# The last output store of a fused attention and MLP block, split by partitions over two DMA queues

## Chip, cores and metric

The kernel runs on one core of a Trainium2 chip. The metric is the device time of one execution in microseconds (us). The kernel before takes 205.89 us (median of three runs, 205.84 to 206.03).

## What is computed

The input `x` has 2048 tokens (S) of width 640 (D), in bf16. It is normalised, and the output is the sum of the input, a linear attention block with 32 heads and an MLP with 1536 hidden columns (F):

```python
xn = _layernorm(x, axis=-1)
return x + _A_ref(xn, A_wqkv, A_wo) + _B_ref(xn, B_w1, B_b1, B_w2, B_b2)
...
# _A_ref
q, k, v = qkv[0], qkv[1], qkv[2]
phi = lambda t: jnp.where(t > 0, t + 1, jnp.exp(t)) + 1e-6
pq, pk = phi(q), phi(k)
kv = jnp.einsum("bhsd,bhse->bhde", pk, v)
z = jnp.einsum("bhsd->bhd", pk)
num = jnp.einsum("bhqd,bhde->bhqe", pq, kv)
den = jnp.einsum("bhqd,bhd->bhq", pq, z)[..., None] + 1e-6
o = num / den
return (lambda x, *d: x.transpose(*d))(o, 0, 2, 1, 3).reshape(B, S, D) @ wo
...
# _B_ref
h = jnp.einsum("bsd,df->bsf", x, w1) + b1
h = _gelu(h)
return jnp.einsum("bsf,fd->bsd", h, w2) + b2
```

## The kernel before

Tokens are worked on in 16 tiles (`t`) of 128, four tiles to a chunk (`c`). The stages follow one another on TensorE: layer norm and the hidden layer of the MLP (line 408 and around), the features of the keys (563, 569), their products with the tokens (596, 605), the features of the queries (648), the matrices that join attention and output weights (658, 702), the denominators (712), and the output.

The output stage is what the change touches. For a tile, `out_mm` (matmuls on line 768) sums 17 products into one PSUM bank: 12 blocks of the hidden layer (`HG`) with `W2`, and 5 blocks of the query features (`PQ`) with the joined matrices (`Msb`). The columns of the output are cut in two: the main part, columns 0 to 511 (`MW` = 512), has the tokens on the partitions; the remainder, 128 columns, is computed transposed for a whole chunk (`rem_mm`, line 779; `rem_done`, line 784), turned back by a DMA transpose and stored from SP. `main_done` (lines 790 to 794) adds the residual to the main part of a tile with one VectorE addition (line 792) into one of two slots of `out_sb`, which is stored by a DMA on ACT's queue, 128 KB.

The order is written out by hand. The remainder of the last chunk comes before its tiles, so that tile 15 is last. Its main part is cut in two pieces, columns 0 to 383 and 384 to 511, each with its own 17 matmuls in a bank of its own, its own addition (line 847) and its own store (line 850). Both stores are issued on SP's queue.

A small recorder, `Planner`, keeps for each engine the list of its operations in program order, and for each buffer part the event of its last writer and of its readers; it makes an engine wait for just those events that it has not yet been seen to know. Each DMA has a semaphore of its own, complete at 16. Every DMA is issued by the helper `dma`, on line 261, or `dma_t`, on line 264, so all issues carry these two line numbers. After the last store, lines 852 to 854 make SP wait for the last DMA of ACT's queue and the last three of its own:

```python
for q, n in ((s_, 1), ("sync", 3)):
    for ev in [ev for (waits, fns, ev, dma_) in Pl.records[q] if dma_][-n:]:
        Pl.wait_event("sync", ev)
```

These waits appear under line 108. After them all engines meet in a closing barrier, shown under the last line of the block, 861. The name `s_` is ACT ("scalar"), and `P` is 128.

Of the kernel before, what the change touches and what calls it, by code (L numbers as in the profile page):

```python
# [7 lines left out]
P = 128  # L8
# [104 lines left out]
def bass_parallel_sum__linear_attn_block__dense_activation_gelu__prompt_kernel(  # L113
# [27 lines left out]
    with contextlib.ExitStack() as es:  # L141
# [46 lines left out]
        out_sb = W1f[:, 2 * DT * D:2 * DT * D + 2 * D].rearrange("p (s d) -> p s d", s=2)  # L188
# [21 lines left out]
        def bank(b, lo=0, hi=512):  # L210
            return ps[:, b * 512 + lo: b * 512 + hi]
# [39 lines left out]
        ov = out.rearrange("b s d -> (b s) d")  # L251
# [5 lines left out]
        s_ = "scalar"  # L257
        pe = "tensor"

        def dma(eng, dst, src, writes, reads=()):  # L260
            Pl.ins(eng, lambda e: e.dma_start(dst, src), reads=reads, writes=writes, dma=True)  # L261
# [12 lines left out]
        for i, (lo, hi) in enumerate(((0, XA), (XA, D))):  # L274
# [21 lines left out]
               reads=[r_ident], writes=[r_ident])  # L296
# [155 lines left out]
        for b in range(6):  # L452
            Pl.ins(pe, lambda e, b=b: e.matmul(
                bank(b), nc.const_aps.tensor(1.0, [P, P], BF16), pm[:].broadcast_to((P, 512)), start=True, stop=False),
                reads=[r_pm], writes=[B_[b]])
# [102 lines left out]
        for c in range(NC):  # L558
            ts = range(c * CH, c * CH + CH)
            cc = slice(c * CW, (c + 1) * CW)  # L560
            for t in ts:
# [4 lines left out]
                    reads=r_xnT[t] + [r_Wk], writes=[B_[b]])  # L566
# [5 lines left out]
                reads=sum((r_xnT[t] for t in ts), []) + [r_Wk], writes=[B_[b]])  # L572
            phi(bank(b), b, 1, PKT[:, cc], r_PKT[c], [])
            dma_t("sync", PK[:, c * CH:(c + 1) * CH, MW:D], PKT[:, cc], [r_PKr[c]] + sum((r_x[t] for t in ts), []),
                  reads=[r_PKT[c]])
# [12 lines left out]
        for k in range(DT):  # L588
            for i in range(DT):
                Pl.ins(g, lambda e, k=k, i=i: e.tensor_copy(plain(Wqkv[:, k, D:2 * D], i), parts(Wqkv[:, k, 0:D], i)),  # L590
                       reads=[r_Wq], writes=[r_Wk, r_WqP])
# [173 lines left out]
        def out_mm(t, lo, hi, w0, w1):  # L765
            seq = seq_of(t)
            for i in range(lo, hi):
                Pl.ins(pe, [(lambda e, i=i, x=x, bk=bk: e.matmul(  # L768
                    bank(bk, 0, x[1] - x[0]), seq[i][0], seq[i][1][:, x[0]:x[1]],
                    start=(i == 0), stop=(i == NS - 1))) for x, bk in zip(w0, w1)],  # L770
                    reads=seq[i][2], writes=[B_[bk] for bk in w1], mark=(i in (JT - 1, NS - 1)))
# [68 lines left out]
        t = NT - 1  # L840
        xb(t)
        tok = slice(t * P, (t + 1) * P)
        for i, (lo, hi, b) in enumerate([(0, 3 * P, bb[1]), (3 * P, MW, bb[2])]):
            r_o = R_("ol%d" % i)
            out_mm(t, 0, NS, [(lo, hi)], [b])
            s = t % 2
            Pl.ins(v, lambda e, lo=lo, hi=hi, b=b: e.tensor_tensor(  # L847
                out=out_sb[:, s, lo:hi], in0=bank(b, 0, hi - lo), in1=x_res[:, t, lo:hi], op=ALU.add),
                reads=[B_[b], r_xb[t]], writes=[r_o] + ([r_out[s]] if i == 0 else []))
            dma("sync", ov[tok, lo:hi], out_sb[:, s, lo:hi], [], reads=[r_o])  # L850

        for q, n in ((s_, 1), ("sync", 3)):
            for ev in [ev for (waits, fns, ev, dma_) in Pl.records[q] if dma_][-n:]:
                Pl.wait_event("sync", ev)

# [35 lines left out]
```

## Time and profile before

| what | before |
|---|---|
| median of three runs | 205.89 us (205.84 to 206.03) |
| the profiled execution's own time | 206.18 us |
| its span, first to last instruction | 204.5 us |
| granted TensorE clock | 1.000 |
| TensorE matmul busy | 200.7 us (98%) |
| VectorE busy | 108.8 us (53%) |
| ScalarE (ACT) busy | 71.3 us (35%) |
| last store, columns 384 to 511 of tile 15: issue to landing | 1.5 us, 32 KB |
| store before it, columns 0 to 383: issue to landing | 1.6 us, 96 KB |
| store of a main part on ACT's queue: issue to landing | 1.7 us, 128 KB |

The profile is one execution. Its own time is the span plus what lies around it. PE is TensorE, DVE is VectorE, ACT is ScalarE, SP is the engine that only issues DMAs and waits; ACTq and SPq are the queues of DMA-issuing instructions of these engines. The times of rows in a timeline count from the start of the span. "Issue" is the instruction that starts a DMA; its data move afterwards on 16 DMA engines, and "landing" is when its semaphore is complete. In the table of DMA queues, q1 holds the transfers that SP issued, q10 those that ACT issued.

### The profile page before, as it was taken

The page shows a single profiled execution, that of the slowest core. Times are in us where ns is not written, and L with a number is a line of the kernel's source. Part 1 is how long each engine was busy: PE and PEld are TensorE (multiplying, and loading weights), DVE is VectorE, ACT ScalarE, POOL GpSimd, SP SyncE. Part 2 cuts the span into 40 slices and gives each one's busy share as a digit, 9 for nine tenths or more (in the row PEclk, how much of TensorE's full clock was granted, in tenths as well). Part 3 has the DMA queues.
Part 4 walks back from the last instruction along what each step waited for, and adds up shares of the span by engine and source line. Part 5 has one row for each costly group of instructions (what it writes and reads, how often), then busy time and mean ns, then how long its engine had stood idle before and what let it go on. Part 6 is the DMA issues. An engine that isn't in the chain of part 4 may idle for free.

```text
span 204.5 us, 3358 instructions
## 1 busy us (share of the span) xinstructions
PE 200.7 (98%) x1238; PEld 104.6 (51%) x1238; DVE 108.8 (53%) x238; ACT 71.3 (35%) x144; POOL 33.5 (16%) x84
## 2 busy tenths in 40 slices
PE   8899999999999999999999999999999999999995
PEld 3899884444444444444546444544444444444443
DVE  3588764000007889399748888834634723513131
ACT  2269995666676555121154464500000000000000
POOL 3245637300000001897000200000000000000000
PEclk9999999999999999999999999999999999999999
DMA  5997595799800111100050001239985511102301
GB/s 170 370 265 93 116 179 101 216 329 353 282 7 0 26 26 26 29 0 0 0 99 2 0 0 21 86 52 201 326 217 131 140 42 52 51 26 51 79 29 51
DMA packets 35769, 21.70 MB, mean 106 GB/s; under 512 B 22696, under 2 KB 35112, under 8 KB 35752
## 3 DMA queue, kind: packets, MB, share of 16 engines
q1 hardware_dynamic: 31696, 17.86, 33.8%
q10 hardware_dynamic: 4056, 3.61, 6.6%
q8 instruction: 10, 0.16, 0.4%
q14 instruction: 7, 0.06, 0.1%
HBM read 13.08 MB, written 2.62 MB: 77 GB/s over the span
## 4 chain that ended last, share of the span: by engine, by line
PE 96%; DMA 2%; SPq 0%; DVE 0%; issue 0%
PE ps L768 29%; PE ps L408 19%; PE ps L648 11%; PE ps L596 8%; PE ps L563 8%; PE ps L779 7%; PE ps L439 3%; PE ps L423 3%; DMA W<-in_B_w_dram 2%; PE ps L605 2%; PE ps L569 2%; PE ps L702 1%; PE ps L658 1%; PE ps L712 1%; SPq L261 0%; DVE W L847 0%
## 5 line engine op out<-in xcount | busy, mean ns | idle before, releaser
L768 PE MATMUL ps<-W,HG 128*128 128x512 bf16 (+2 forms) x204 | 43.9, 367 | 0.0
L408 PE MATMUL ps<-xnT,W 128*128 128x512 bf16 (+1 forms) x225 | 39.1, 336 | 0.0
L768 PEld LDWEIGHTS ps<-W,HG 128*128 128x128 bf16 x204 | 19.5, 98 | 22.2 <-ACT Msb L684 0.2
L551 ACT ACTIVATE ek<-ps 128x512 bf16<-128x512 f32 x40 | 23.8, 597 | 19.6 <-DVE PQ L554 9.3
L408 PEld LDWEIGHTS ps<-xnT,W 128*128 128x128 bf16 x225 | 21.9, 98 | 16.8 <-issue 0.3
L412 ACT ACTIVATE HG<-ps,b1c 128x512 bf16<-128x512 f32 (+1 forms) x45 | 26.3, 670 | 11.3 <-PE ps L408 10.8
L552 DVE TENSOR_SCALAR ek<-ek 128x512 bf16<-128x512 bf16 x40 | 11.4, 286 | 28.3 <-ACT ek L551 28.3
L792 DVE TENSOR_TENSOR W<-ps,xnT 128x512 bf16<-128x512 f32 x15 | 10.4, 691 | 24.9 <-PE ps L768 19.6
L648 PE MATMUL ps<-xnT,Wqkv 128*128 128x512 bf16 x100 | 21.9, 379 | 0.0
L768 PE MATMUL ps<-Msb,PQ 128*128 128x512 bf16 (+2 forms) x85 | 19.6, 366 | 0.0
L563 PE MATMUL ps<-Wqkv,xnT 128*128 128x512 bf16 x80 | 17.9, 379 | 0.0
L596 PE MATMUL ps<-xPK,xn_tm 128*128 128x512 bf16 x80 | 17.4, 379 | 0.0
L590 POOL COPY Wqkv<-Wqkv 128x128 bf16<-128x128 bf16 x25 | 13.5, 540 | 22.4 <-PE ps L569 20.9
L357 DVE BATCH_NORM_STATS2 stats<-xPK 128x6 f32<-128x320 bf16 (+2 forms) x32 | 13.9, 478 | 5.3 <-DMA xPK<-in_A_x_dram 5.3
L648 PEld LDWEIGHTS ps<-xnT,Wqkv 128*128 128x128 bf16 x100 | 9.6, 98 | 11.5
L554 DVE SCALAR_TENSOR_TENSOR PQ<-ps,ek 128x512 bf16<-128x512 f32 x20 | 13.8, 691 | 2.1
L768 PEld LDWEIGHTS ps<-Msb,PQ 128*128 128x128 bf16 x85 | 8.1, 98 | 9.2
L596 PEld LDWEIGHTS ps<-xPK,xn_tm 128*128 128x128 bf16 x80 | 7.8, 98 | 9.4
L563 PEld LDWEIGHTS ps<-Wqkv,xnT 128*128 128x128 bf16 x80 | 7.8, 98 | 9.4
L554 DVE SCALAR_TENSOR_TENSOR xPK<-ps,ek 128x512 bf16<-128x512 f32 x16 | 11.1, 692 | 1.7
L619 DVE TENSOR_TENSOR Msb<-Msb,xPK 128x640 f32<-128x640 f32 x14 | 11.6, 826 | 0.5
L367 POOL TENSOR_TENSOR rstd<-aggr,mhalf 128x1 f32<-128x1 f32 x16 | 10.0, 623 | 7.4 <-DVE aggr L365 7.4
(77 smaller groups left out, 156.6 us busy)
## 6 DMA issues: line engine op xcount, KB each, us to landing
Wqkv<-in_A_wqkv_dram SPq DMA_DIRECT2D x3, 800.0 KB, 6.8
xnT<-in_A_x_dram SPq DMA_DIRECT2D x4, 512.0 KB, 6.5
W<-in_B_w_dram SPq DMA_DIRECT2D x5, 384.0 KB, 5.6
W<-in_B_w_dram SPq DMA_DIRECT2D x1, 1920.0 KB, 13.4
out_dram<-W ACTq DMA_DIRECT2D x15, 128.0 KB, 1.7
xn_tm<-rden ACTq DMA_DIRECT2D x12, 128.0 KB, 3.8
xPK<-in_A_x_dram SPq DMA_DIRECT2D x4, 320.0 KB, 6.9
Wo<-in_A_wo_dram SPq DMA_DIRECT2D x8, 160.0 KB, 8.9
```

Of the source, the lines that this page charges most:

```text
L357: Pl.ins(v, lambda e: e.bn_stats(stats[:, s, 6 * h:6 * h + 6], x_in[:, t, lo:hi]), reads=[r_x[t][min(h, len(r_x[t]) - 1)]], writes=[r_stat ...
L408: Pl.ins(pe, [(lambda e, k=k: e.matmul(bank(b, 0, w), W1[:, k, jb * P:(jb + 1) * P], xnT[:, k, tok], start=(k == 0), stop=(k == DT - 1))) ...
L412: Pl.ins(s_, lambda e: e.activation(HG[:, jb, tok], bank(b, 0, w), ACT.Gelu_apprx_tanh, bias=b1c[:, jb:jb + 1]), reads=[B_[b], r_b1c], wri ...
L551: Pl.ins(s_, lambda e: e.activation(e2, src, ACT.Exp), reads=br, writes=[r_ek[s]])
L554: Pl.ins(v, lambda e: e.scalar_tensor_tensor(out=d2, in0=src, scalar=0.0, in1=e2, op0=ALU.max, op1=ALU.add), reads=br + [r_ek[s]], writes= ...
L563: Pl.ins(pe, [(lambda e, k=k, b=b, t=t: e.matmul(bank(b), xnT[:, k, t * P:(t + 1) * P], Wqkv[:, k, D:D + MW], start=(k == 0), stop=(k == D ...
L590: Pl.ins(g, lambda e, k=k, i=i: e.tensor_copy(plain(Wqkv[:, k, D:2 * D], i), parts(Wqkv[:, k, 0:D], i)), reads=[r_Wq], writes=[r_Wk, r_WqP])
L596: Pl.ins(pe, lambda e, t=t, b=b, f=f, i=i: e.matmul(bank(b), xn_tm[:, t, f * P:(f + 1) * P], PK[:, t, 0:MW], start=(i == 0), stop=(i == NT ...
L619: Pl.ins(v, lambda e, t=t: e.tensor_tensor(out=zsum, in0=zsum, in1=PK[:, t, :], op=ALU.add), reads=[r_PK[t], r_PKr[t // CH], r_zsum], writ ...
L648: Pl.ins(pe, [(lambda e, k=k, j=j, b=b: e.matmul(bank(b), Wqkv[:, k, D + j * P:D + (j + 1) * P], xnT[:, k, cc], start=(k == 0), stop=(k == ...
L768: Pl.ins(pe, [(lambda e, i=i, x=x, bk=bk: e.matmul(bank(bk, 0, x[1] - x[0]), seq[i][0], seq[i][1][:, x[0]:x[1]], start=(i == 0), stop=(i = ...
L779: Pl.ins(pe, lambda e, i=i: e.matmul(bank(b), seq[i][0], seq[i][1], start=(i == 0), stop=(i == NS - 1)), reads=seq[i][2], writes=[B_[b]], ...
```

## The change

The store of the last piece (columns 384 to 511 of tile 15) becomes two stores of 64 partitions each: partitions 0 to 63 on SP's queue, partitions 64 to 127 on ACT's queue. Both read the result of the same addition. The store of columns 0 to 383 stays on SP's queue, whole. The waits at the end take the last two DMAs of ACT's queue, so that the new one is among them.

```diff
                 reads=[B_[b], r_xb[t]], writes=[r_o] + ([r_out[s]] if i == 0 else []))
-            dma("sync", ov[tok, lo:hi], out_sb[:, s, lo:hi], [], reads=[r_o])
-
-        for q, n in ((s_, 1), ("sync", 3)):
+            if i == 0:
+                dma("sync", ov[tok, lo:hi], out_sb[:, s, lo:hi], [], reads=[r_o])
+            else:
+                for q, r0 in (("sync", 0), (s_, P // 2)):
+                    dma(q, ov[t * P + r0:t * P + r0 + P // 2, lo:hi], out_sb[r0:r0 + P // 2, s, lo:hi], [], reads=[r_o])
+
+        for q, n in ((s_, 2), ("sync", 3)):
             for ev in [ev for (waits, fns, ev, dma_) in Pl.records[q] if dma_][-n:]:
                 Pl.wait_event("sync", ev)
```

On each engine the program is otherwise the same: SP's last issue has 64 rows instead of 128, ACT's queue has one more issue of 64 rows at its end, and the other engines' instructions are unchanged.

## The prediction

> **What bounds the kernel now.** I read the chain of waits first. TensorE carries it nearly to the end:
>
> ```profile
> PE 96%; DMA 2%; SPq 0%; DVE 0%; issue 0%
> ...
> 187.44 14.73 PE ps L768 x85
> 202.17 0.02 issue
> 202.19 0.29 DVE W L847
> ```
>
> The change touches no matmul, so only what follows the last matmul can move. Next, the timeline of the last 3.5 us (columns: start us, us, engine, line, operation):
>
> ```profile
> 201.25 0.56 DVE L847 TENSOR_TENSOR W<-ps,xnT 128x384 bf16<-128x384 f32 x1 [1.74 <-PE ps L768]
> 201.71 0.44 PE L768 MATMUL ps<-Msb,PQ 128*128 128x128 bf16 x5
> 201.83 1.02 SPq L261 DMA_DIRECT2D out_dram<-W  x2
> 202.19 0.29 DVE L847 TENSOR_TENSOR W<-ps,xnT 128x128 bf16<-128x128 f32 x1 [0.39 <-PE ps L768]
> ```
>
> The two SP issues are shown as one row. The view of line 261 gives the length of one, and when the second starts:
>
> ```profile
> L261 SPq DMA_DIRECT2D out_dram<-W x2: 344/344/345, 201.8 to 202.5; - x2
> ```
>
> So the first runs from 201.83 to 202.18, and the second ends at 201.83 + 1.02 = 202.85 and starts 0.344 earlier, at 202.51, within 0.03 us of the end of the last addition at 202.48. The data of the stores are not in these rows; a table by stage over the tail has them (last two columns: share of the 16 DMA engines, GB/s):
>
> ```profile
> 202.67:203.12 0.45, 0.00 (x0) 0.00 (x0) 0.00 (x0) 0.00 (x0) 0.00 (x0) 1.00 0.68 219
> 203.12:203.35 0.23, 0.00 (x0) 0.00 (x0) 0.00 (x0) 0.00 (x0) 0.00 (x0) 1.00 0.00 0
> 203.35:203.62 0.27, 0.00 (x0) 0.00 (x0) 0.00 (x0) 0.00 (x0) 0.00 (x0) 1.00 0.56 122
> 203.62:204.45 0.83, 0.00 (x0) 0.00 (x0) 0.00 (x0) 0.00 (x0) 0.00 (x0) 1.00 0.00 0
> ```
>
> The first active stretch is the 96 KB store, the second the 32 KB store. The wait at the end shows when SP learns that each has landed:
>
> ```profile
> L108 SPq EVENT_SEMAPHORE  x2: 17/22/28, 203.5 to 204.0; - x2
> ```
>
> The tail of the store that the change splits is therefore: issue at 202.51; 0.84 us without a packet, up to 203.35; 0.27 us of packets, up to 203.62; 0.37 us until SP passes the last wait at 203.99; 0.46 us of closing barrier up to 204.45. Only 0.27 us of these 1.94 us is movement of data; the rest does not depend on how many bytes one queue carries.
>
> **What the Trainium skill says.** (1) "DMA: Bandwidth & Descriptors", section "Rules for kernel authors": two transfers to disjoint partition halves are not worth it, since both spread over the same 16 DMA engines. No run here shows this shape yet; the trace agrees in that all 16 engines take part in the 32 KB store (its 128 rows show as 144 packets: the rows and 16 small ones that end each engine's share). (2) The same page, section "Why a DMA increments its semaphore by 16 and not by 1": the number of engines is the largest divisor, up to 16, of the slowest dimension; 64 rows still give 16 engines, four rows on each. (3) "Perfetto Trace Analysis", section "DMA Instruction — HWDGE (DVE, Sync)": the two issuing sequencers share one descriptor generator, which one holds at a time. The trace has a pair that agrees in part, used below.
>
> **The change part by part.** The sum is made against the profiled execution: 206.18 us, of which 204.45 us is the span and 1.73 us lies around it. It is 0.29 us above the median of 205.89 us, so I add differences to the median.
>
> *SP's half.* The SP instruction stays where it was, with 64 rows in place of 128. Its issue of 0.344 us hardly depends on rows: a store of 512 rows takes 0.377 to 0.387 us. From these, 64 rows fewer save under 0.01 us. The issue itself has not been what the end waits for, since packets start 0.84 us after its start. SP's half should then start packets at 203.35 as before.
>
> *ACT's half, added.* ACT has been idle since its last store:
>
> ```profile
> 199.21 0.34 ACTq L261 DMA_DIRECT2D out_dram<-W  x1
> ```
>
> That one was released by the addition that ended at 198.48 + 0.69 = 199.17, so ACT starts 0.04 us after its addition where SP took 0.03: the new issue starts at 202.52, 0.01 behind SP's, and ends at 202.86. No instruction waits behind it on ACT but the closing barrier, which ACT then reaches at 202.9 instead of 199.6; SP reaches it at 204.0, so this is covered by 1.1 us. Alone, an ACT store's first packet comes at 200.05, 0.84 us after its issue, the same as on SP. At the same time as SP's, it may be later. The trace has one such pair among the stores, at 191.80 and 191.87:
>
> ```profile
> 191.80 0.38 SPq L261 DMA_DIRECT2D out_dram<-xPK  x1
> 191.87 0.34 ACTq L261 DMA_DIRECT2D out_dram<-W  x1
> ```
>
> Neither issue is lengthened. The DMA queues show which one's packets come first, in the stretches 192.60 to 192.84 and 192.60 to 192.86:
>
> ```profile
> q1 hardware_dynamic: 90, 0.02, 40.8%
> ```
>
> ```profile
> q1 hardware_dynamic: 105, 0.03, 43.9%
> q10 hardware_dynamic: 3, 0.00, 3.3%
> ```
>
> q1 is SP's, q10 ACT's. Until 192.84 there is nothing from ACT; its first packets come at 192.85, 0.98 us after its issue and 0.14 us after SP's first (192.71). The pair at the very start of the kernel, issued within 0.01 us of each other at 0.81, says the same: SP's first packet at 1.85, ACT's at 1.99, again 0.14 us later. So the price of a simultaneous issue is bounded by 0 (two generators) and 0.14 us (the second of the pair waits its turn). I take 0.14, since both pairs show it, and keep 0 as the other end.
>
> *The packets*, read one by one from the trace's packet records. Within the 32 KB store each of 16 engines moves 8 rows; the first engine is done at 203.47 (0.11 us after the first packet), the last at 203.61. The spread of 0.14 us between engines is there for stores of 96 and 128 KB too (0.16 us), so I keep it. Four rows instead of eight take 0.06 us instead of 0.11. ACT's half: first packet 203.35 + 0.14 = 203.49, last 203.49 + 0.06 + 0.14 = 203.69, against 203.61 before: +0.08 us. SP's half is over by 203.55 and does not decide. On any one engine SP's four rows are gone by the time ACT's four arrive (0.06 against 0.14 us), so they don't queue on each other. With no offset between the halves an engine would move the same eight rows plus one more small closing packet of 0.01 us, and the first packet may come 0.01 earlier with fewer rows: between -0.01 and +0.01 us.
>
> *The end.* The landing follows the last packet by 0.36 us and does so for the 128 and 96 KB stores also (0.35); kept. SP now waits for five semaphores instead of four. As built, the second of its two wait instructions takes the two halves together, and the first one the older stores, so no instruction is added: 0. The wait that is added for the older ACT store has been over since 200.9 (199.21 + 1.7 us to its landing). The barrier keeps its 0.46 us.
>
> *Sum.* +0.08 us: the span goes to 204.53, the profiled execution to 206.26, and the median to 205.89 + 0.08 = 205.97 us.
>
> **The rivals.** *A, offset (the forecast):* 205.97, as above, within 0.2% (0.41 us, about what a measurement of this kernel can tell from no change).
>
> *B, both halves at once:* the skill's lock does not show because each issue needs the generator only briefly. Both queues start at 203.35 and finish with the old store, 205.88 to 205.90, or down to 205.84 if an engine moves the rows of its two queues side by side, so that each saves 0.05 us. The pair at 191.80 and the one at 0.81 speak against it; two records are few. It can't become a gain beyond 0.2%: even if all 0.27 us of packets vanished, the time would be 205.62, which is still within it. That the split does nothing at all is this case too.
>
> *C, the lock lengthens an issue:* slower than before. While ACT was issuing its broadcasts around 140 us, SP's loads took far longer to issue:
>
> ```profile
> L261 ACTq DMA_DIRECT2D xn_tm<-rden x5: 635/825/1369, 139.2 to 142.4; - x5
> L261 SPq DMA_DIRECT2D xnT<-in_A_x_dram x3: 368/822/855, 139.5 to 140.9; - x3
> ```
>
> One took 0.368 us, two took 0.82 to 0.86. If one half has to wait like this at its issue, its packets and its landing are later by 0.855 - 0.368 = 0.49 us, and the median is 205.89 + 0.49 = 206.38, or 206.46 with A's 0.08. It decides "slower" from 0.41 us on, so only a delay of nearly this size counts. Against it: DMA engines[...] were full of broadcasts and loads at 140 us and are empty at 202.5, and neither issue of the pair at 191.80 (0.377 and 0.344 us) was lengthened.
>
> **How the numbers follow.** A 0.72, B 0.20, C 0.08. The likeliest is A, so 205.97 is the forecast. A's own range is +0.02 to +0.15 us (offset smaller for fewer rows, or the whole 0.14 without the rows saved); B adds the lower end, -0.05 us. The three runs of before span 0.19 us; I allow half of that, 0.10, below, and above it the 0.14 by which the highest run exceeds the median. Lower end: 205.89 - 0.05 - 0.10 = 205.74; upper end: 205.89 + 0.15 + 0.14 = 206.18. C is left outside, with A and B's own tails no more than 2 in 10. Chances: faster by over 0.2% is only measurement, 0.02; slower by over 0.2% is C, 0.08 less the part of it under 0.41 us, so 0.07; within 0.2% 0.91.
>
> **What would show it.** In the profile after: SP's and ACT's issue both at 202.5 on this clock, each of about 0.34 us (right for A and B; over 0.8 for one of them is C). Packets of q1 from 0.84 us after the issue, those of q10 0.14 us later (A) or together (B). Last packet 0.08 us later against the end of the last addition (A) or within 0.02 (B). Two wait instructions on SP as before, and 0.46 us from the last to the end of the span. The prediction is wrong if the gap from the last packet to the landing is not 0.36 us with two queues, if ACT starts late because it was idle for 3 us, or if the matmuls before the tail move at all.

## The result and the profile after

The changed kernel is slower: 206.85 us (median of six runs, 206.76 to 207.16) against 206.00 for the kernel before beside it (six runs, 205.84 to 206.40). The ratio is 1.0040, 95% interval 1.0027 to 1.0053, so 0.56 to 1.09 us. The forecast was 205.97 us, with a range up to 206.18; the time lies above it.

The profiled execution took 206.82 us with a span of 205.1 us, against 206.18 and 204.5. The chain of waits is less tidy than before, because 17 matmul records are missing from this trace (1221 matmuls in place of 1238) and the chain goes round the gaps by other engines; its last piece is the same work with the same end, TensorE up to 202.2 us:

```profile
PE 72%; DVE 19%; DMA 4%; issue 2%; ACT 1%; DVEq 0%
...
196.16 6.05 PE ps L768 x44
```

The end of the last addition moved by 0.04 us, from 202.49 to 202.53. In the profiles of the kernels below it lies anywhere between 201.99 (e8) and 202.83 (g4), so this shift says nothing of the change. The rest of the 0.62 us by which the span grew lies behind it. The timeline of the tail, and the view of line 261 there (minimum, median and maximum length in ns):

```profile
201.87 1.24 SPq L261 DMA_DIRECT2D out_dram<-W  x2
202.23 0.29 DVE L847 TENSOR_TENSOR W<-ps,xnT 128x128 bf16<-128x128 f32 x1 [0.39 <-PE ps L768]
202.56 0.57 ACTq L261 DMA_DIRECT2D out_dram<-W  x1
```

```profile
L261 SPq DMA_DIRECT2D out_dram<-W x2: 345/451/557, 201.9 to 202.6; - x2
L261 ACTq DMA_DIRECT2D out_dram<-W x1: 575/575/575, 202.6 to 202.6; - x1
```

The 96 KB store is issued in 0.345 us as before. The two halves take 0.557 and 0.575 us, where the whole store took 0.344. The table by stage shows the same delay in the data (last two columns: share of the DMA engines, GB/s):

```profile
202.70:203.16 0.46, 0.00 (x0) 0.00 (x0) 0.00 (x0) 0.00 (x0) 0.00 (x0) 1.00 0.67 214
203.16:203.75 0.59, 0.00 (x0) 0.00 (x0) 0.00 (x0) 0.00 (x0) 0.00 (x0) 1.00 0.00 0
203.75:203.99 0.24, 0.00 (x0) 0.00 (x0) 0.00 (x0) 0.00 (x0) 0.00 (x0) 1.00 0.33 69
203.99:204.02 0.03, 0.00 (x0) 0.00 (x0) 0.00 (x0) 0.00 (x0) 0.00 (x0) 1.00 0.00 0
204.02:204.26 0.24, 0.00 (x0) 0.00 (x0) 0.00 (x0) 0.00 (x0) 0.00 (x0) 1.00 0.34 69
204.26:205.08 0.82, 0.00 (x0) 0.00 (x0) 0.00 (x0) 0.00 (x0) 0.00 (x0) 1.00 0.00 0
```

The silence between the 96 KB store and the last piece was 0.23 us and is 0.59. The queues in the stretch from 203.74 to 204.03 say whose packets came first:

```profile
q1 hardware_dynamic: 80, 0.02, 27.7%
q10 hardware_dynamic: 1, 0.00, 0.3%
```

SP's half (q1, 64 rows and 16 closing packets) is complete before ACT's (q10) begins. And SP's last wait, which began at 204.0 and lasted 28 ns, now begins when SP's half has landed and is held 268 ns for ACT's:

```profile
L108 SPq EVENT_SEMAPHORE  x2: 28/148/268, 203.5 to 204.4; - x2
```

In terms of the prediction's sum, counted from the end of the last addition: SP's first packet at 1.23 us instead of 0.87 (+0.36); ACT's first packet 0.27 behind it; packets of one half 0.22 us instead of 0.26 (-0.04); landing 0.36 after the last packet, as before (counted, here and below, from the start of that packet, a closing one of 0.01 us). Together +0.59, and the span does end 2.55 us after the addition where it ended 1.97 us after it.

### The profile page after: what moved, and what is told of

Read it like the earlier page. It is cut to its first block, busy times and chain, and to the rows that moved or that the text cites. A ratio compares the mean times of both kernels' runs of the same rounds, so it can differ in the third digit from the quotient of the medians.

```text
span 205.1 us, 3342 instructions
## 1 busy us (share of the span) xinstructions
PE 200.2 (98%) x1221; PEld 105.0 (51%) x1238; DVE 108.8 (53%) x238; ACT 71.3 (35%) x144; POOL 33.4 (16%) x84
## 4 chain that ended last, share of the span: by engine, by line
PE 72%; DVE 19%; DMA 4%; issue 2%; ACT 1%; DVEq 0%
PE ps L768 29%; PE ps L408 19%; PE ps L779 7%; PE ps L563 6%; DVE Msb L619 6%; DVE PQ L554 3%; PE ps L439 3%; PE ps L423 3%; PE ps L648 3%; DVE ek L552 2%; DVE xPK L554 2%; DMA Msb<-Msb 2%; DMA xPK<-Msb 1%; DMA xPK<-in_A_x_dram 1%; PE ps L569 1%
```

## The experiments

Two questions were open: why the issues and first packets of the halves are late, and why ACT's comes 0.27 us after SP's. The table gives, for all kernels, how long an issue takes, and then times in us counted from the end of the last addition, from the packet and landing records of their profiles. The last two columns are how much later than before the span ends in this count ("tail"), and the difference of the medians of the runs, each against the kernel before as run beside it. The ratios in the text are estimates from all these runs, and not quotients of the medians: for g4 they differ most (1.0001, and +0.18 us between the medians).

| kernel | issue SP; ACT | first packet SP; ACT | last landing | end of span | tail | medians |
|---|---|---|---|---|---|---|
| before | 0.34; - | 0.87; - | 1.48 | 1.97 | | |
| changed | 0.56; 0.58 | 1.23; 1.50 | 2.08 | 2.55 | +0.59 | +0.85 |
| e4, SP half only | 0.56; - | 1.23; - | 1.81 | 2.31 | +0.34 | +0.47 |
| e1, both on SP | 0.56, 0.59; - | 1.23, 1.87; - | 2.44 | 2.92 | +0.96 | +1.02 |
| e6, whole stores as a pair | 0.34; 0.35 | 0.95; 0.89 | 1.85 | 2.34 | +0.37 | +0.38 |
| e2, by columns | 0.35; 0.37 | 0.87; 0.94 | 1.63 | 2.10 | +0.14 | +0.13 |
| e7, 96 and 32 rows | 0.35; 0.38 | 0.88; 0.96 | 1.65 | 2.11 | +0.14 | +0.29 |
| e8, four quarters | 0.35, 0.42; 0.38, 0.45 | 0.87, 1.34; 0.91, 1.38 | 2.08 | 2.61 | +0.65 | +0.88 |
| e3, late ACT | 0.55; 0.55 | 1.23; 1.53 | 2.11 | 2.57 | +0.61 | +0.71 |
| changed, again | 0.56; 0.58 | 1.23; 1.50 | 2.07 | 2.54 | +0.58 | +0.69 |
| g1, whole, unmarked | 0.56; - | 1.23; - | 1.85 | 2.35 | +0.38 | +0.42 |
| g2, 96 and 32, unmarked | 0.63; 0.62 | 1.30; 1.57 | 2.10 | 2.56 | +0.59 | +0.82 |
| g3, 80 and 48 rows | 0.35; 0.38 | 0.88; 0.95 | 1.63 | 2.11 | +0.14 | +0.13 |
| g4, 120 and 8 rows | 0.41; 0.32 | 0.93; 0.84 | 1.51 | 2.00 | +0.04 | +0.18 |

Each tail lies within the 95% interval of its own comparison, which reaches 0.14 to 0.28 us to either side. The medians are on average 0.1 us above the tails, and in the first comparison 0.26 us; that part is not explained.

**First theories: a collision of two issues, or the 64 rows.** The rival that the prediction had named, a lock that lengthens an issue, would need two issues at once. So one half was left out.

```diff
-                for q, r0 in (("sync", 0), (s_, P // 2)):
+                for q, r0 in (("sync", 0),):
...
-        for q, n in ((s_, 2), ("sync", 3)):
+        for q, n in ((s_, 1), ("sync", 3)):
```

> Only SP's half of the last piece is stored (64 rows); the store of partitions 64 to 127 of the last 128 columns of tile 15 is left out. Theory 'rows': a 64-row store is dearer by itself. Then its issue takes 0.56 us as in the changed kernel, its first packet comes 1.20 us after the issue, and the time is 0.3 us above the kernel before. Theory 'collision': two issues at the same moment hold each other up, and 64 rows cost nothing. Then the issue takes 0.34 us, the first packet comes after 0.84 us, and the time is that of the kernel before, less up to 0.05 us.

```profile
L261 SPq DMA_DIRECT2D out_dram<-W x2: 344/450/557, 201.6 to 202.3; - x2
```

```profile
202.90:203.50 0.60, 0.00 (x0) 0.00 (x0) 0.00 (x0) 0.00 (x0) 0.00 (x0) 1.00 0.00 0
203.50:203.73 0.23, 0.00 (x0) 0.00 (x0) 0.00 (x0) 0.00 (x0) 0.00 (x0) 1.00 0.35 72
```

With nothing on ACT the issue of 64 rows still takes 0.557 us, and the silence is still 0.60 us. The ratio is 1.0022 (1.0013 to 1.0032). A store of half the data is slower than the whole one: the collision is out as the cause of the 0.36 us.

Both halves on one queue:

```diff
-                for q, r0 in (("sync", 0), (s_, P // 2)):
+                for q, r0 in (("sync", 0), ("sync", P // 2)):
...
-        for q, n in ((s_, 2), ("sync", 3)):
+        for q, n in ((s_, 1), ("sync", 4)):
```

> Both 64-row halves on SP's queue, one after the other, so that no two issues meet. 'Rows': each issue 0.56 us, the second half's first packet 0.56 + 1.20 us after the addition; the time is 0.9 us above the kernel before. 'Collision': each issue 0.34 us, second half 0.34 us later than the old store, the time 0.3 us above.

Issues of 0.557 and 0.586 us, one after the other; ratio 1.0042 (1.0030 to 1.0055), +1.02 us between the medians and +0.96 of tail, where "rows" had said 0.9.

A pair of whole 128-row stores, the 96 KB one held back to the second addition (this edit is shown against the kernel before; the waits are those of the changed kernel):

```diff
-            dma("sync", ov[tok, lo:hi], out_sb[:, s, lo:hi], [], reads=[r_o])
+            if i == 0:
+                r_o0 = r_o
+            else:
+                dma("sync", ov[tok, 0:lo], out_sb[:, s, 0:lo], [], reads=[r_o0, r_o])
+                dma(s_, ov[tok, lo:hi], out_sb[:, s, lo:hi], [], reads=[r_o])
```

> No split: the 96 KB store (SP) is held back to the second addition, so that it and the 32 KB store (now on ACT) of 128 rows each are issued at the same moment. 'Collision': both issues about 0.56 us, first packets at 1.2 us (SP) and 1.47 us (ACT) after the issue, the time 0.6 us or more above the kernel before. 'Rows': both issues 0.34 us, first packets at 0.84 and 0.98 us, the time 0.15 to 0.3 us above.

The issues started 0.04 us apart and took 0.344 and 0.349 us. First packets came 0.86 us (ACT) and 0.88 us (SP) after their issues. Ratio 1.0019 (1.0011 to 1.0026), a little above what "rows" had expected: with both stores on the way at once the packets go on until 1.48 us after the addition, where those of the 32 KB store alone ended at 1.13. No collision of the issues here either, and the first packets are 0.07 us apart, not 0.14. The split by columns:

```diff
-                for q, r0 in (("sync", 0), (s_, P // 2)):
-                    dma(q, ov[t * P + r0:t * P + r0 + P // 2, lo:hi], out_sb[r0:r0 + P // 2, s, lo:hi], [], reads=[r_o])
+                for q, c0 in (("sync", lo), (s_, lo + 64)):
+                    dma(q, ov[tok, c0:c0 + 64], out_sb[:, s, c0:c0 + 64], [], reads=[r_o])
```

> The last piece is split by columns instead of partitions: 128 rows of 64 columns (128 bytes) each on SP's and ACT's queue at the same moment. 'Collision': issues of 0.56 us and the time 0.6 us above the kernel before, as in the changed kernel. 'Rows': issues of 0.34 us, ACT's packets 0.14 us after SP's, the time 0.1 to 0.15 us above.

The same bytes, over the same two queues, at the same moment, and the ratio is 1.0006 (0.9998 to 1.0015). ACT's packets come 0.06 us after SP's, not 0.14. The pair costs 0.14 us of tail; the rest of the changed kernel's 0.59 was now put down to the 64 rows.

**Fewer rows, or 64?** The next theory was that every store of fewer than 128 rows pays.

```diff
-                for q, r0 in (("sync", 0), (s_, P // 2)):
-                    dma(q, ov[t * P + r0:t * P + r0 + P // 2, lo:hi], out_sb[r0:r0 + P // 2, s, lo:hi], [], reads=[r_o])
+                for q, r0, r1 in (("sync", 0, 96), (s_, 96, P)):
+                    dma(q, ov[t * P + r0:t * P + r1, lo:hi], out_sb[r0:r1, s, lo:hi], [], reads=[r_o])
```

> The split is uneven: 96 partitions on SP's queue, 32 on ACT's. Theory 'flat': every store of fewer than 128 rows pays the same, 0.56 us of issue and 1.20 us to its first packet, and the second of a pair comes 0.27 us after the first. Then both issues take 0.56 to 0.58 us and the time is that of the changed kernel within 0.05 us. Theory 'by rows': the price goes with the rows or with the rows on each of 16 engines (6 and 2 here). Then SP's issue lies between 0.34 and 0.56 us and ACT's is above 0.6.

```profile
L261 SPq DMA_DIRECT2D out_dram<-W x2: 345/348/350, 201.6 to 202.3; - x2
L261 ACTq DMA_DIRECT2D out_dram<-W x1: 377/377/377, 202.3 to 202.3; - x1
```

Both theories failed: neither 96 nor 32 rows are dear (0.350 and 0.377 us of issue; ratio 1.0011, 1.0004 to 1.0018). Four quarters say so again:

```diff
-                for q, r0 in (("sync", 0), (s_, P // 2)):
-                    dma(q, ov[t * P + r0:t * P + r0 + P // 2, lo:hi], out_sb[r0:r0 + P // 2, s, lo:hi], [], reads=[r_o])
+                for q, r0 in (("sync", 0), (s_, 32), ("sync", 64), (s_, 96)):
+                    dma(q, ov[t * P + r0:t * P + r0 + 32, lo:hi], out_sb[r0:r0 + 32, s, lo:hi], [], reads=[r_o])
...
-        for q, n in ((s_, 2), ("sync", 3)):
+        for q, n in ((s_, 3), ("sync", 4)):
```

> The suspected cost doubled: four stores of 32 partitions, two on each queue. 'Flat', with one generator that serves the stores in turn: the second store of each queue is issued 0.56 to 0.6 us after the first, and the last first packet comes about 2.1 us after the addition where it was 1.50 in the changed kernel; the time is 0.5 us above the changed kernel, 1.1 above the kernel before. If the four are prepared side by side, the time is at most 0.1 us above the changed kernel.

```profile
L261 SPq DMA_DIRECT2D out_dram<-W x3: 344/352/416, 201.3 to 202.4; - x3
L261 ACTq DMA_DIRECT2D out_dram<-W x2: 378/412/445, 202.0 to 202.4; - x2
```

Issues of 0.35 to 0.45 us instead of 0.56, and the last first packet at 1.38 us instead of 2.1: "flat" fails in its parts. The ratio is 1.0043 (1.0030 to 1.0057), which is 0.6 to 1.2 us, and the tail is 0.06 us above the changed kernel's. It is that long for another reason: the last packet comes at 1.56 us, earlier than in the changed kernel (1.72), and the last landing 0.52 us after it instead of 0.36. This is taken up below.

**In turn?** ACT's half was delayed:

```diff
+                Pl.ins(s_, lambda e: e.activation(ek[:, 0, 0:64], HG[:, 0, 0:64], ACT.Copy),
+                       reads=[r_o], writes=[r_ek[0]])
-                for q, r0 in (("sync", 0), (s_, P // 2)):
+                for q, r0, rd in (("sync", 0, [r_o]), (s_, P // 2, [r_o, r_ek[0]])):
```

(`rd` replaces `[r_o]` in the stores' reads.)

> As the changed kernel, but ACT's half is issued about 0.3 us after SP's: a copy of 64 columns to an unused buffer on ACT stands between the addition and that store. Theory 'in turn': ACT's packets come 0.27 us after SP's because one generator works on SP's half first. Then the delay hides in that wait, ACT's first packet stays at 1.5 us after the addition, and the time is that of the changed kernel within 0.06 us. Theory 'slow queue': the 0.27 us belong to ACT's queue or to the upper partitions. Then they are added to the delay, and the time is 0.3 us above the changed kernel.

```profile
L261 ACTq DMA_DIRECT2D out_dram<-W x1: 551/551/551, 202.8 to 202.8; - x1
```

ACT's issue started 0.29 us later than in the changed kernel, and its first packet only 0.03 us later (1.53 against 1.50); ratio 1.0035 (1.0023 to 1.0047), beside 1.0037 for the changed kernel. Its first packet came 1.22 us after its issue, as SP's does (1.20). So the 0.27 us belong neither to ACT's queue nor to the upper partitions: ACT's half waits while SP's is prepared, and a delay of that size is free. This is what the one shared generator that the prediction cites would do; no run looks into it.

**The changed kernel once more.**

> The changed kernel once more, beside these. The tail after the last addition is 0.59 us longer in its profile than in the kernel before (0.35 us to the first packet, 0.27 offset of ACT's half, -0.04 of packets). If that is all, the time is 0.6 us above the kernel before; if something outside the tail adds to it, it is 0.8 us above as in the first comparison.

Ratio 1.0037 (1.0024 to 1.0050), 0.69 us between the medians, tail +0.58. The expected 0.6 and 0.8 us are both inside this interval (0.49 to 1.03 us): it agrees with the tail, and does not exclude another 0.1 to 0.2 us from elsewhere.

**What 64 rows lack.** In the built program, the list of instructions made from the kernel's text, the 64-row stores differ from those of 128, 96 and 32 rows in one field besides their sizes and places. The builder had set a mark, `ant_dge_precooked`, on the others and not on these. Twelve more copies in this program lack it: ACT's broadcasts around 140 us, which in the trace of the kernel before took

```profile
L261 ACTq DMA_DIRECT2D xn_tm<-rden x12: 613/742/1369, 134.8 to 143.8; - x12
```

against 338 for ACT's marked stores from 152 us on. (Two marked stores close behind the broadcasts, at 144.8 and 145.5, took 647 and 607 as well, so a long issue alone does not show that the mark is missing.) The mark can be withheld for one instruction. First from the last store of the kernel before, which is otherwise left as it was:

```diff
+        def dma_u(eng, dst, src, writes, reads=()):
+            def issue(e):
+                nc.dge_precook = False
+                r = e.dma_start(dst, src)
+                nc.dge_precook = True
+                return r
+            Pl.ins(eng, issue, reads=reads, writes=writes, dma=True)
...
-            dma("sync", ov[tok, lo:hi], out_sb[:, s, lo:hi], [], reads=[r_o])
+            (dma, dma_u)[i]("sync", ov[tok, lo:hi], out_sb[:, s, lo:hi], [], reads=[r_o])
```

> The kernel before, with one thing changed on its last store: the mark that the builder puts on nearly every DMA instruction of this program, and does not put on a store of exactly 64 rows, is taken off it. 128 rows, SP's queue, no split. Theory 'mark': the price of the 64-row stores is that of an instruction without the mark. Then the issue takes 0.56 us, the first packet comes about 1.2 us after it, and the time is 0.36 us above the kernel before. Theory '64': the price belongs to 64 rows on 16 engines, four each, whatever the instruction carries. Then the issue takes 0.34 us, the first packet comes after 0.84 us, and the time is that of the kernel before.

The unmarked store is recorded under its own line, 266:

```profile
L266 SPq DMA_DIRECT2D out_dram<-W x1: 562/562/562, 202.5 to 202.5; - x1
```

```profile
203.14:203.74 0.60, 0.00 (x0) 0.00 (x0) 0.00 (x0) 0.00 (x0) 0.00 (x0) 1.00 0.00 0
203.74:204.02 0.28, 0.00 (x0) 0.00 (x0) 0.00 (x0) 0.00 (x0) 0.00 (x0) 1.00 0.54 117
```

The issue takes 0.562 us and the silence 0.60 us, with 128 rows, one queue and no split. Ratio 1.0019 (1.0010 to 1.0028), tail +0.38. As built, this kernel differs from the kernel before in the mark of this one store and in nothing else. Then from both parts of the split 96 and 32, with `dma_u` for `dma` in e7's edit:

> The split 96 and 32, with the mark taken off both stores. 'Mark': issues of 0.56 to 0.58 us, SP's first packet 1.2 us after its issue and ACT's about 0.27 us behind it, the time 0.6 us above the kernel before, as in the changed kernel. '64': as the split 96 and 32 with the mark, 0.14 us above.

```profile
L266 SPq DMA_DIRECT2D out_dram<-W x1: 629/629/629, 202.8 to 202.8; - x1
L266 ACTq DMA_DIRECT2D out_dram<-W x1: 616/616/616, 202.8 to 202.8; - x1
```

Issues of 0.63 and 0.62 us, somewhat longer than "mark" had said, ACT's first packet 0.27 us behind SP's, tail +0.59, ratio 1.0035 (1.0022 to 1.0047): the changed kernel's loss without a 64-row store. No run gives a 64-row store the mark, but little is left for the rows themselves: the first packet comes at 1.23 us both for 64 rows (e4) and for 128 unmarked ones (g1). Last, the nearest marked relative of the changed kernel, e7's edit with 80 in place of 96:

> The nearest marked relative of the changed kernel: 80 partitions on SP's queue and 48 on ACT's. 'Mark': issues of 0.35 to 0.38 us, first packets 0.85 and 0.93 us after the issues, the time 0.14 us above the kernel before. '64' in its wider form, that four rows or so on an engine are dear (here five and three): issues between 0.4 and 0.56 us, the time 0.3 us or more above.

```profile
L261 SPq DMA_DIRECT2D out_dram<-W x2: 345/348/352, 201.7 to 202.4; - x2
L261 ACTq DMA_DIRECT2D out_dram<-W x1: 378/378/378, 202.4 to 202.4; - x1
```

Issues of 0.35 and 0.38 us, tail +0.14, ratio 1.0007 (0.9998 to 1.0015). That is the price of such a split with the mark.

**The last 0.1 us of a marked split.** In e2, e7 and g3 the last landing follows the last packet by 0.46 to 0.48 us, not 0.36. The profile records each of the 16 increments of a store's semaphore, up to the 16 that SP waits for. In e2 and g3 those of SP's store land first and all of ACT's after them (SP's 1.30 to 1.47 us, ACT's 1.49 to 1.63 in g3); in e7 the two groups overlap by 0.01 us.

> The split 120 and 8, so that the two stores use 15 and 8 DMA engines and complete with 15 and 8 increments instead of 16 and 16. Theory 'one at a time': in the marked splits the last 0.1 us comes from 32 increments that arrive about 0.011 us apart, so that ACT's land after all of SP's. Then ACT's 8 increments take about 0.09 us instead of 0.17, and the last landing is about 0.08 us earlier than with 96 and 32. Theory 'late queue': ACT's completion is late by itself, and the last landing stays 0.15 to 0.18 us after SP's. The time is 0.05 to 0.15 us above the kernel before either way.

The edit is e7's with 120 in place of 96. The run does not show what makes the last 0.1 us. With 8 rows ACT's store was ready first (first packet 0.84 us, SP's 0.93), and its increments were over by 1.25 us, before SP's began at 1.41. The two never met, the last landing came 0.34 us after the last packet, and the tail is +0.04 (ratio 1.0001, 0.9990 to 1.0012). ACT's 8 increments took 0.05 us, not the 0.09 of "one at a time". "Late queue" does not hold: ACT's landing came 0.26 us before SP's, and 0.34 us after its own last packet; in the changed kernel, e3 and g2, where ACT's packets are the last and alone, its landing follows them by 0.36 us too. What is left is that completions hold each other up when they meet. It fits e2, e7, g3 and e8; how they would do so is not shown.

## Why the prediction was wrong

The step that failed is the first of its sum, "SP's half": its issue "hardly depends on rows", and SP's packets "start at 203.35 as before". I had drawn a line through stores of 512 and 128 rows and read 64 off it. The quantity was not on that line: as built, the 64-row stores belong to another kind of instruction, which takes 0.56 instead of 0.34 us to issue and 1.20 instead of 0.84 us to its first packet (e4, and g1 without any change of rows). This is +0.36 us, set at less than 0.01, out of the 0.51 us between the +0.08 of the sum and the +0.59 of the tail. Part of the evidence was at hand. The broadcasts quoted for rival C took about twice as long to issue as most stores, and I put that down to traffic. But the first two of them met none: no packet moved between 130.0 and 136.1 us, and the first packet of the first came 1.29 us after its issue.

```profile
L261 ACTq DMA_DIRECT2D xn_tm<-rden x2: 613/628/643, 134.8 to 135.5; - x2
...
134.80:136.09 1.29, 1.29 (x7) 0.59 (x6) 0.00 (x0) 0.00 (x0) 0.00 (x0) 1.00 0.00 0
```

*ACT's half.* Right in its start (0.03 us after the addition, though ACT had been idle) and in its cover at the barrier. The offset was of the right kind and mis-sized: 0.14 us was taken, from pairs of other shapes (a store of 512 rows, loads at the start), 0.27 us measured between these halves, and 0.06 to 0.09 us between marked ones (e2, e7, g3). This is the other 0.13 us of the miss. The offset goes with the mark: with 96 and 32 rows it is 0.09 us with it (e7) and 0.27 without (g2). That it is the time for which the first of the pair is prepared fits e3, but was not measured apart.

*Packets.* Right: -0.04 us measured, -0.05 expected.

*The end.* Right: landing 0.36 us after the last packet, no instruction added to SP's waits (the fifth wait is for ACT's half; the older ACT store was waited for before too), and the end of the span 0.47 us after the last landing (0.48 before). It was right only because the halves landed apart; in the marked splits, where they land together, the 0.36 becomes 0.46 to 0.48.

*The rivals.* A's mechanism is there, inside a larger loss. B is excluded for these halves: their first packets are 0.27 us apart. C had the right sign and place, an issue that gets longer, and the wrong reason: one half alone takes 0.557 us to issue (e4), as it does beside the other. It was priced at 0.49 us, given 0.08, and left outside the range; that its total came near the measured loss is luck.

With marked stores the tail would have been some +0.14 us, judging by g3, instead of the forecast +0.08, and still within 0.2%. What took the time out of the range is the mark, in both terms.

The Trainium skill's advice against two transfers on partition halves ("DMA: Bandwidth & Descriptors", section "Rules for kernel authors"), cited in the prediction, holds in every split by partitions run here: none was faster, and the best was +0.04 us of tail. Its reason, shared DMA engines, is not what decided: the packets of a half are 0.22 us of 2.55, and each half had the engines to itself.

## What to carry to other kernels

A last store of 32 KB is almost all latency, here 0.84 us to the first packet, 0.36 to the landing and 0.5 of barrier, so splitting it can save at most part of 0.26 us of packets, and adds a second issue, whose packets come later, and a second completion. Before a DMA's shape is changed, see how the new instruction is built, not only its rows and bytes, and compare the issue times of the kinds of DMA that the profile already has; a class of issues at twice the time of the others, where no other transfer is in the way, is a warning. Two points of a price do not bound a third that may be of another kind.

## What was not expected of the hardware

- With identical rows, queue and data, a DMA instruction without the builder's mark took 0.56 us instead of 0.34 us to issue, and its first packet came 1.20 us instead of 0.84 us after the start of the issue. Of the row counts tried in the last store, 64 alone lacked it; 8, 32, 48, 80, 96, 120 and 128 had it.
- Two stores issued within 0.01 us of each other sent their first packets 0.04 to 0.10 us apart when marked (e8's first two, e2, e7, g3; in g4 it was the store issued second, of 8 rows, that came first), and 0.27 us when not.
- The 16 increments of a last store arrived over 0.14 to 0.20 us, and over 0.22 and 0.23 us in e6 (g4, whose stores have fewer such increments, left aside). When the packets of two stores ended within 0.1 us of each other (e2, e7, g3), the last landing came 0.10 to 0.12 us later after the last packet than for a single store, and with four stores (e8) 0.16 us later.
